# Down matmuls and small transforms as crossed pairs of 64-row halves

## The chip, the cores and the metric

The kernel runs on one core of a Trainium2 chip, in one launch. The metric is the device time of that launch in microseconds, as the median of several runs; before the change it is 916.47 us (three runs, 916.1 to 916.57). All matmul operands are bf16, all sums are kept in float32 in PSUM. The engines are called as the profile calls them: PE (TensorE), PEld (its weight loads), DVE (VectorE), ACT (ScalarE), POOL (GpSimd), SP (which issues DMAs).

## What is computed

A sequence of 2048 tokens with 576 channels passes through two layers, each of which is a long-convolution block A and then a gated feed-forward block B, both with a residual:

```python
def _A_ref(q, k, v, shift_k, ssm_k, ssm_D):
    k_shift = ...            # causal 4-tap filter of k, by channel
    kv = k_shift * v
    y = ...                  # causal convolution of kv with ssm_k over 2048 steps (by FFT)
    y = y + kv * ssm_D[None, None, :]
    return q * y

def _B_ref(x, w_gate, w_up, w_down):
    return (_gelu(x @ w_gate) * (x @ w_up)) @ w_down

x = A_q
x = x + _A_ref(_layernorm(x, axis=-1), A_k, A_v, A_shift_k, A_ssm_k, A_ssm_D)
x = x + _B_ref(_layernorm(x, axis=-1), B_w_gate, B_w_up, B_w_down)
x = x + _A_ref(_layernorm(x, axis=-1), A_k, A_v, A_shift_k, A_ssm_k, A_ssm_D)
x = x + _B_ref(_layernorm(x, axis=-1), B_w_gate, B_w_up, B_w_down)
```

The gate and up matrices are 576 x 4608, the down matrix 4608 x 576. The convolution's result does not depend on the layer's input, so it is computed once and used in both layers.

## The kernel before

**Units, passes and visits.** The tokens are cut into four chunks of 512 (four rows of 128). A unit is one layer on one chunk; there are eight, in five passes (`passes = [[0], [1, 2], [3, 4], [5, 6], [7]]`, L750). The 4608 hidden columns are cut into three phases of 12 tiles of 128. A visit is one phase of one unit, 24 visits in all (loop from L1569). In each visit PE first runs gate/up and then down.

**Gate/up** (`gu`, L1038): the contraction over 576 channels is cut into nine blocks of 64. Gate's block lies on partitions 0 to 63 and up's on 64 to 127, so a gate matmul of 64 rows and an up matmul of 64 rows run side by side in the two halves of the array, each 512 columns long and into its own PSUM bank. For each of the 12 tiles `fi` this is nine pairs. ACT then applies gelu, DVE multiplies and writes `hT` (L1619 to L1629).

**Down** (loop from L1643): for each of the four rows `j` and each tile `fi`, two matmuls of the full 128 rows and 288 columns (the two halves `h` of the 576 outputs, `down`, L1650) accumulate in a tile of two PSUM banks. A row is finished before the next is begun. Its result is added to the residual by DVE, in `plus` (queued in `late`, L1698) or directly for the second layer's last phase.

**PSUM.** There are four tiles of two banks (L760). Three are handed out in turn by `pr` (L784), which notes in `bank_at` when each will be free; the fourth belongs to the convolution's transforms, which may also borrow one of the three (`other`, `conv.alt`).

**Transforms.** While the units run, the convolution of chunks 1 to 3 is worked off beside them: the Fourier transforms are small matmuls on PE, `quarter` (L307) and `fwd_eo` (L295) forward and `inverse` (L347) back, each with 128 rows and 288 columns. ACT or DVE evicts them (the forward ones into `eo`, of which there are few), DVE combines them (`cross`, L318). They stand in the queue `Pq` and are issued by `run_p` (L709) within `fill` (L1099).

**The order of work** is written by the program itself: it keeps a clock for PE, DVE and ACT (`Pace`), with a fixed cost for every kind of operation (constants at L32 to L43), and issues each piece of other work into the engines' queues when the clocks say that it fits. `fill` is called after every gate/up tile and after every down tile; it issues loads, evictions, gate and norm steps on DVE (`run_vq`, L1007) and ACT (`run_aq`, L894), convolution work on DVE and transforms on PE. Between gate/up tiles a transform is issued only if two can go together or it has been skipped twice (`pair_ready`, L699), and then `C_TURN = 0.2` us is added to PE's clock (L1641). `pressing` (L1093) says that the next unit's input is due soon. Each engine runs its instructions in the order in which they were issued; waits between engines are semaphores that the framework derives from the tiles read and written.

The normalised rows of a unit are transposed either by a DMA on SP's queue (`spread`) or on PE (`turn_row`, L1049).

Of the kernel before, what the change touches and what calls it, by code (L numbers as in the profile page):

```python
# [17 lines left out]
P = 128  # L18
# [3 lines left out]
RT = BS // P  # L22
HW = 288
# [3 lines left out]
NEVER = 1e9  # L27
# [6 lines left out]
C_P0, C_P1, C_AC = 1.28, 1.35, 0.7  # L34
C_TT, C_ST, C_BN, C_NORM, C_HT, C_GELU, C_EVA, C_EVD, C_YH = 0.69, 0.75, 0.47, 0.62, 0.615, 0.51, 0.56, 0.69, 0.7
C_HB = 0.345
C_FOLD = 0.38
C_TURN = 0.2
LAG = 0.25
AHEAD = 2.0  # L40
SLOW, PRESS = 6.0, 22.0
NAT = 22.0
HOLD, SOON, QUIET, LEAD, FAR = 18.0, 30.0, 10.0, 1.8, 3.6  # L43
# [91 lines left out]
class Conv:  # L135
# [9 lines left out]
    def __init__(self, tc, ctx, pace, gwork, xtp, A_k, A_v, A_shift_k, A_ssm_k, A_ssm_D, ident, cps, ypool):  # L145
# [40 lines left out]
        self.left = 0  # L186
        self.spills = deque()

# [106 lines left out]
    def fwd_eo(self, src, kt, s, h, ring, scale=1.0):  # L295

        nc = self.nc
        ps = self.ps()
        for e in range(2):
            for i in (e, e + 2):  # L300
                nc.tensor.matmul(ps[:, e, 0:HW], lhsT=self.fw(kt, s, i),  # L301
                                 rhs=src(i)[:, h * HW:(h + 1) * HW], start=(i == e), stop=(i == e + 2))
        eo = self.eo_tile(ring)
        nc.scalar.activation(out=eo[:], in_=ps[:, :, 0:HW], func=ACT.Copy, scale=scale)
        return eo

    def quarter(self, src, e, s, h, ring, scale=1.0):  # L307

        nc = self.nc
        ps = self.ps()  # L310
        for n, i in enumerate((e, e + 2)):
            nc.tensor.matmul(ps[:, n, 0:HW], lhsT=self.fw(0, s, i), rhs=src(i)[:, h * HW:(h + 1) * HW], start=True, stop=True)  # L312
        eo = self.eo_tile(ring)
        nc.scalar.activation(out=eo[:], in_=ps[:, :, 0:HW], func=ACT.Copy, scale=scale)  # L314
        return eo
# [31 lines left out]
    def inverse(self, m, mt, terms):  # L347
        nc = self.nc
        if m not in self.y:
            self.y[m] = self.ypool.tile([P, RT, self.D], BF16, tag="y", name="y")  # L350
        ps = self.ps()
        for n, (lhs, z) in enumerate(terms):
            for h in range(2):
                nc.tensor.matmul(ps[:, h, 0:HW], lhsT=lhs, rhs=z[:, h * HW:(h + 1) * HW],  # L354
                                 start=(n == 0), stop=(n == len(terms) - 1))
        return self.halves(self.y[m][:, mt, :]), ps[:, :, 0:HW]
# [19 lines left out]
    def step(self, m, kv=None, loaded=False):  # L376
# [74 lines left out]
        def fwd(kt, s, h):  # L451
            def run():
                if s == 0 and h == 0:
                    for k in (kt, kt + 2):
                        kc[k] = self.kcp.tile([P, 2, D], BF16, tag="kc", name="kc")
                free, ring = self.eo_free(True)
                eo = self.fwd_eo(lambda i: self.vt_[m][:, i, :], kt, s, h, ring)
                done = t.on_act(C_EVA, max(t.pe + 0.49 + LAG, self.eo_at[ring].popleft()))
                self.ps_free[self.cur] = done
                if (kt, s, h) == (1, 1, 1):  # L460
                    self.fwd_at[m] = t.pe + 0.49
# [109 lines left out]
        def fwd4(filt, e, s, h):  # L571
# [3 lines left out]
            def run():  # L575
                free, ring = self.eo_free(m == 1)
                eo = self.quarter(src, e, s, h, ring, scale)
                done = t.on_act(C_EVA, max(t.pe + 0.25 + LAG, self.eo_at[ring].popleft()))
                self.ps_free[self.cur] = done
                if last:  # L580
                    (self.hf_at if filt else self.fwd_at)[m] = t.pe + 0.25
                    if filt and loaded:
                        self.hr_free[0] = self.hr_free[1] = self.hf_at[m]
# [63 lines left out]
        def inv(mt):  # L647
            def run():
                self.yb = nyb
                cost = 0.49  # L650
                out, in_ = self.inverse(m, mt, [(self.V_[:, s, mt, :], w[mt, s]) for s in range(2)])
# [6 lines left out]
                self.ps_free[self.cur] = done + LAG  # L658
                self.y_at[(m, mt)] = done + LAG
            return run  # L660
# [48 lines left out]
    def run_p(self):  # L709
# [10 lines left out]
        self.Pq.popleft()  # L720
        run()
        t.pe += cost
        if self.cur:
            self.borrowed(self.ps_free[1])
        return True

@with_exitstack
def ssm_geglu_kernel(ctx, tc, A_q, A_k, A_v, A_shift_k, A_ssm_k, A_ssm_D, B_x, B_w_gate, B_w_up,
# [165 lines left out]
    def run_aq(limit):  # L894
        only = coming[0] if pressing() else None
        found = [(prio, n) for n, (prio, ready, cost, run, ui) in enumerate(aq) if (only is None or ui == only) and ready() <= t.pe]
        if not found:
            return False
        n = min(found)[1]
        cost, run = aq[n][2:4]  # L900
        if max(t.act, t.pe - 1.0) + cost > limit:
            return False
        del aq[n]
        run()
        return True
# [101 lines left out]
    def run_vq(limit):  # L1007
# [7 lines left out]
        else:  # L1015
            r = NEVER if len(xn_made) >= 3 or not xn_open() else need[1].get("rstd_at", NEVER)
        if r > t.pe + 0.2 or max(t.dve, t.pe - 1.0) + cost > limit:
            return False
# [50 lines left out]

    conv.borrowed = lambda when: bank_at.__setitem__(taken[0] % 3, when)  # L1070
    conv.alt_at = lambda: bank_at[(taken[0] + 1) % 3]
# [26 lines left out]

    def fill(limit, tensor, conv_first, between=None):  # L1099
        weights()  # L1100
        conv.run_loads()
        spreads(tensor=tensor)
        while True:
            if run_late(limit):
# [31 lines left out]
    with tc.manual_schedule():  # L1136
# [432 lines left out]
        for at, (wb, ph, ui, first, final) in enumerate(visits):  # L1569
            coming[0], due_at[0] = ui, t.pe  # L1570
            layer, c = units[ui]
            while xn_done.get(ui, 0) < RT:
                if xn_made and xn_made[0][3] - 0.3 <= t.pe:
                    turn_row(*xn_made.popleft())
# [67 lines left out]
            ahead[:] = [t.pe + RT * FP * C_DN, visits[at + 1][2] if at + 1 < len(visits) else None]  # L1642
            for j in range(RT):  # L1643
                acc = pr("dn")
                mine = taken[0]
                conv.alt = other
                xa = x_c[c][:, j, :]
                xh = xa.rearrange("p (h d) -> p h d", h=2)

                def down(fi, h, acc=acc):  # L1650
                    nc.tensor.matmul(acc[:, h, 0:HW], lhsT=hT[:, fi, j * P:(j + 1) * P],  # L1651
                                     rhs=wd[2 * wb + fi // WT][:, fi % WT, h * HW:(h + 1) * HW],
                                     start=(fi == 0), stop=(fi == FP - 1))
                if wb == NWB - 1 and j == RT - 1:
                    dst = out2[c * CH:(c + 1) * CH, :].rearrange("(p j) d -> p j d", j=RT)[:, j, :]
                    for h in range(2):
# [7 lines left out]
                        nc.sync.dma_start(out=dst[:, h * HW:(h + 1) * HW], in_=ob[:, 0:HW])  # L1664
                    break
                for fi in range(FP):
                    for h in range(2):
                        down(fi, h)
                    t.pe += C_DN
                    if fi < FP - 1:  # L1670
                        fill(t.pe + 1.5, True, conv.left > 0)
                if layer == 1 and end:
                    ob, entry = out_tile()
# [9 lines left out]
                else:  # L1683
                    def plus(c=c, j=j, layer=layer, ph=ph, end=end, acc=acc, xa=xa, xh=xh):
# [11 lines left out]
                        if layer == 0 and end:  # L1696
                            vq.extend(prep(units.index((1, c)), j))
                    late.append((t.pe + 0.2, mine, plus))  # L1698
        conv.flush(NEVER)

# [49 lines left out]
```

## Time and profile before

| | |
|---|---|
| median of three runs | 916.47 us |
| profiled execution | 916.83 us |
| its span, first to last instruction | 915.1 us |
| granted TensorE clock in the profiled execution | 1.0 |
| instructions in the span | 19163 |
| PE matmuls | 8051 |
| bytes moved by DMA | 128.81 MB, mean 141 GB/s |

The profile is of one execution. A row of its groups gives the line and engine, the output and inputs by the program's names, the shape and count, then the busy time in us, the mean duration of one in ns, and the idle time before them with what ended it. Matmuls overlap in the pipeline: one of 288 columns lasts 286 ns from start to end, and the next begins long before that, so the pitch from one to the next has to be taken from a stretch of many. In shapes, `64*128 64x512` is a matmul that uses 64 rows and 128 columns of the array and streams 512 columns. The chain is the sequence of work that ended last, followed back from the end; its pieces are given with start, length and count.

### The profile page before, as it was taken

The page shows a single profiled execution, that of the slowest core. Times are in us where ns is not written, and L with a number is a line of the kernel's source. Part 1 is how long each engine was busy: PE and PEld are TensorE (multiplying, and loading weights), DVE is VectorE, ACT ScalarE, POOL GpSimd, SP SyncE. Part 2 cuts the span into 40 slices and gives each one's busy share as a digit, 9 for nine tenths or more (in the row PEclk, how much of TensorE's full clock was granted, in tenths as well). Part 3 has the DMA queues.
Part 4 walks back from the last instruction along what each step waited for, and adds up shares of the span by engine and source line. Part 5 has one row for each costly group of instructions (what it writes and reads, how often), then busy time and mean ns, then how long its engine had stood idle before and what let it go on. Part 6 is the DMA issues. An engine that isn't in the chain of part 4 may idle for free.

```text
span 915.1 us, 19163 instructions
## 1 busy us (share of the span) xinstructions
PE 907.8 (99%) x8051; PEld 522.5 (57%) x8051; DVE 565.0 (62%) x1131; ACT 364.7 (40%) x679; POOL 148.4 (16%) x311
## 2 busy tenths in 40 slices
PE   9999999999999999999999999999999999999998
PEld 7746556465565564655655655646646546556555
DVE  8888987774889886578887833543333334433332
ACT  7774446535435366254244233441121224321211
POOL 5443003320113012231023001210000002100000
PEclk9999999999999999999999999999999999999999
DMA  9999967449619606986944700882720820877630
GB/s 245 307 250 271 247 157 127 128 135 230 200 53 231 140 1 98 253 131 161 240 143 92 167 16 27 145 154 57 139 78 1 155 79 14 150 164 179 134 101 27
DMA packets 125819, 128.81 MB, mean 141 GB/s; under 512 B 40866, under 2 KB 118051, under 8 KB 125732
## 3 DMA queue, kind: packets, MB, share of 16 engines
q1 hardware_dynamic: 116706, 92.63, 47.8%
q0 software_dynamic: 8880, 34.36, 11.9%
q8 instruction: 63, 1.03, 0.5%
q10 hardware_dynamic: 146, 0.59, 0.2%
q14 instruction: 24, 0.20, 0.1%
HBM read 106.91 MB, written 11.80 MB: 130 GB/s over the span
## 4 chain that ended last, share of the span: by engine, by line
PE 93%; DVE 4%; ACT 1%; issue 1%; POOL 1%; DMA 0%; ACTq 0%; DVEq 0%; SPq 0%
PE gu L1041 57%; PE dn L1651 30%; PE ps L284 1%; PE cps L312 1%; DVE kvt L255 1%; PE cps L354 1%; DVE kvt L261 1%; PE ps L1273 0%; PE cps L301 0%; DVE x_c L925 0%; DVE hT L1629 0%; PE ps L1408 0%; DVE hT L1621 0%; PE ps L1041 0%; DVE hh L610 0%
## 5 line engine op out<-in xcount | busy, mean ns | idle before, releaser
L1041 PE MATMUL gu<-xnT,wgu 64*128 64x512 bf16 x5148 | 560.6, 376 | 0.9 <-DVE hT L1629 0.6
L1041 PEld LDWEIGHTS <-wgu 64*128 64x128 bf16 x5220 | 252.4, 94 | 306.1 <-issue 7.0
L1651 PE MATMUL dn<-wd,hT 128*128 128x288 bf16 x2304 | 293.9, 286 | 0.0
L1651 PEld LDWEIGHTS <-hT 128*128 128x128 bf16 x2304 | 223.4, 98 | 65.8 <-issue 8.1
L1629 DVE TENSOR_TENSOR hT<-ga,gu 128x512 bf16<-128x512 f32 x169 | 115.7, 686 | 175.6 <-ACT ga L1628 175.5
L1628 ACT ACTIVATE ga<-gu 128x512 f32<-128x512 f32 x169 | 100.5, 595 | 309.4 <-PE gu L1041 305.6
L1619 ACT ACTIVATE ga<-gu 128x512 bf16<-128x512 f32 x117 | 69.8, 597 | 156.4 <-PE gu L1041 143.0
L1621 DVE TENSOR_TENSOR hT<-ga 128x512 bf16<-128x512 bf16 x118 | 49.3, 420 | 57.4 <-ACT ga L1620 57.3
L1620 ACT CAST ga<-gu 128x512 bf16<-128x512 f32 x117 | 67.9, 580 | 0.0
L873 POOL TENSOR_SCALAR means<-s 128x1 f32<-128x1 f32 x28 | 16.0, 573 | 238.1 <-DVE x_c L1687 211.1
L1695 DVE TENSOR_TENSOR x_c<-x_c,dn 128x576 f32<-128x576 f32 x32 | 24.0, 751 | 26.3 <-PE dn L1651 26.1
L1693 DVE SCALAR_TENSOR_TENSOR x_c<-dn,means,x_c 128x576 f32<-128x576 f32 x28 | 22.8, 814 | 26.2 <-PE dn L1651 26.2
L314 ACT ACTIVATE eo<-cps 128x576 f32<-128x576 f32 x40 | 25.3, 657 | 25.1 <-DVE ab L319 9.2
L889 POOL TENSOR_TENSOR rstd<-ve,neghalf_t 128x1 f32<-128x1 f32 x56 | 33.6, 600 | 4.7
L331 DVE TENSOR_TENSOR prod<-prod 128x576 bf16<-128x576 bf16 x64 | 29.3, 458 | 2.2
L1674 DVE TENSOR_TENSOR xn<-x_c,dn 128x576 bf16<-128x576 f32 x15 | 11.3, 753 | 28.0 <-PE dn L1651 28.0
L915 ACT ACTIVATE yh<-y,rstd 128x576 f32<-128x576 bf16 x28 | 21.3, 771 | 10.4 <-DVE x_c L925 8.1
L610 DVE TENSOR_TENSOR kc<-ab,cd 128x288 bf16<-128x288 f32 x64 | 25.2, 449 | 0.0
L873 POOL TENSOR_SCALAR nm<-s 128x1 f32<-128x1 f32 x28 | 9.9, 353 | 94.1 <-DVE x_c L925 94.0
L425 POOL DMA_DIRECT2D kr<-Kd x20 | 11.0, 551 | 83.8 <-DVE prod L330 83.8
L881 ACT ACTIVATE junk<-x_c,nm 128x576 bf16<-128x576 f32 x28 | 21.5, 767 | 4.0 <-POOL nm L873 2.8
L888 POOL TENSOR_SCALAR ve<-ss 128x1 f32<-128x1 f32 x56 | 15.2, 272 | 41.8 <-ACT junk L881 41.6
(177 smaller groups left out, 609.3 us busy)
## 6 DMA issues: line engine op xcount, KB each, us to landing
wgu<-in_B_w_gate_dram SPq DMA_DIRECT2D x45, 576.0 KB, 5.6
wd<-in_B_w_down_dram SPq DMA_DIRECT2D x30, 864.0 KB, 6.7
wgu<-in_B_w_up_dram SPq DMA_DIRECT2D x45, 512.0 KB, 8.3
hr<-Hd POOLq DMA_DIRECT2D x32, 288.0 KB, 5.4
kr<-Kd POOLq DMA_DIRECT2D x24, 288.0 KB, 4.3
Kd<-kc POOLq DMA_DIRECT2D x12, 288.0 KB, 5.9
k<-in_A_k_dram POOLq DMA_DIRECT2D x3, 1008.0 KB, 11.0
wgu<-in_B_w_up_dram SPq DMA_DIRECT2D x45, 64.0 KB, 7.6
```

The lines of the kernel that those rows point to most:

```text
L314: nc.scalar.activation(out=eo[:], in_=ps[:, :, 0:HW], func=ACT.Copy, scale=scale)
L331: nc.vector.tensor_tensor(out=dst[:, cols], in0=pr[:, 0, cols], in1=pr[:, 1, cols], op=ALU.subtract if part == 0 else ALU.add)
L610: nc.vector.tensor_tensor(out=into[k][:, plane, cols], in0=a, in1=b, op=op)
L873: nc.gpsimd.tensor_scalar(out=v["nm"][:], in0=v["s"][:], scalar1=-1.0 / D, scalar2=None, op0=ALU.mult)
L889: nc.gpsimd.tensor_tensor(out=v["rstd"][:], in0=ve[:], in1=neghalf_t[:, 0:1], op=ALU.pow)
L1041: nc.tensor.matmul(cols(pair[:, s, :]), lhsT=w[r0:r0 + HK, k, gi * P:(gi + 1) * P], rhs=cols(xnT[r0:r0 + HK, blk_of[k], :]), start=(k == 0 ...
L1619: nc.scalar.activation(out=ga[:, 0, :], in_=pair[:, 0, :], func=ACT.Gelu_apprx_tanh)
L1620: nc.scalar.copy(out=ga[:, 1, :], in_=pair[:, 1, :])
L1621: nc.vector.tensor_tensor(out=hT[:, fi, :], in0=ga[:, 0, :], in1=ga[:, 1, :], op=ALU.mult)
L1628: nc.scalar.activation(out=ga[:], in_=pair[:, 0, :], func=ACT.Gelu_apprx_tanh)
L1629: nc.vector.tensor_tensor(out=hT[:, fi, :], in0=ga[:], in1=pair[:, 1, :], op=ALU.mult)
L1651: nc.tensor.matmul(acc[:, h, 0:HW], lhsT=hT[:, fi, j * P:(j + 1) * P], rhs=wd[2 * wb + fi // WT][:, fi % WT, h * HW:(h + 1) * HW], start=( ...
```

## The change

Matmuls with 128 contraction rows are split into two of 64 rows each, as gate/up has them. A tile has two output halves in two banks. In step 0 the upper 64 rows go to the first output and the lower 64 to the second, side by side; in step 1 crossed, the lower rows to the first output and the upper to the second. Between the steps a wait is placed: an empty instruction on ACT's sequencer that reads the PSUM tile (`conv.hold`), so that step 1 begins on PE only when step 0 has been written.

```diff
+    def half_rows(self, outs, terms, step):
+        for n, (lhs, rhs) in enumerate(terms):
+            for k in range(2):
+                r = slice((step ^ k) * (P // 2), (step ^ k) * (P // 2) + P // 2)
+                self.nc.tensor.matmul(outs[k], lhsT=lhs[k][r], rhs=rhs[k][r], start=step == 0 and n == 0,
+                                      stop=step == 1 and n == len(terms) - 1)
+
+    def both_steps(self, outs, terms):
+        ps = self.ps()
+        self.half_rows(outs(ps), terms, 0)
+        self.hold(ps)
+        yield
+        self.half_rows(outs(ps), terms, 1)
+        return ps
...
+    conv.hold = lambda ps: nc.scalar.keepalive_nop([nc.scalar.lower_ap(ps[:, :, 0:HW])])
```

`fwd_eo` and `quarter` use it, `inverse` too for chunks 2 and 3 (`m > 1`); for chunk 1 it stays as it was. `run_p` issues step 0 and puts the rest into a list `open`; `run_open`, called at the start of `fill`, issues step 1 when PE's clock is `DRAIN = 0.35` us further. Other matmuls stand between the two.

The down rows go two by two; the last two rows of the last visit stay whole and one by one:

```diff
+            def two_rows(j):
+                order = ([(0, 0, fi) for fi in range(FP - 2)] + [(1, 0, fi) for fi in range(FP - 3)] +
+                         [(0, 0, fi) for fi in range(FP - 2, FP)] + [(1, 0, fi) for fi in range(FP - 3, FP)] +
+                         [(n, 1, fi) for n in range(2) for fi in range(FP)])
+                for k, (n, step, fi) in enumerate(order):
+                    acc, mine = opened(j + n)
...
+                    for g in range(2):
+                        r = slice((step ^ g) * HK, (step ^ g) * HK + HK)
+                        nc.tensor.matmul(acc[:, g, 0:HW], lhsT=lhs[r], rhs=wn[r, g * HW:(g + 1) * HW],
+                                         start=step == 0 and fi == 0, stop=step == 1 and fi == FP - 1)
+                    if step == 0 and fi == FP - 1:
+                        conv.hold(acc)
+                    t.pe += C_DN / 2
+                    if step == 1 and fi == FP - 1:
+                        evict(j + n)
+                    elif k % 2:
+                        conv.alt = other
+                        fill(t.pe + 1.5, True, conv.left > 0)
...
+            two_rows(0)
+            if wb == NWB - 1:
+                conv.alt = None
+                row(2)
+                row(3)
+            else:
+                two_rows(2)
```

So of two rows, the first one's step 0 runs for ten tiles, the second one's for nine, then the first one's last two and the second one's last three, and then step 1 of the first row and of the second.

The planner's numbers and rules change with it: `C_TT` 0.69 to 0.74, `C_ST` 0.75 to 0.80, `C_EVD` 0.69 to 0.72, `C_TURN` 0.2 to 0.0, `SLOW` 6.0 to 5.0, a transform's matmuls count half for each step; between gate/up tiles `pair_ready` is no longer asked; while the next unit is `pressing`, steps of it may be issued up to `NEAR = 2.2` us before they are ready, and `run_aq` is called before DVE's work then and otherwise once instead of repeatedly:

```diff
-        while run_aq(min(limit, t.pe + 2.3)):
-            pass
+        run_aq(min(limit, t.pe + 2.3))
         conv.between = between is not None
-        if tensor and between is not None and not ((1 in conv.z_at or conv.dry(between)) and conv.pair_ready()):
+        if tensor and between is not None and not (1 in conv.z_at or conv.dry(between)):
             return
```

More of the change, by code (lines that the diff above doesn't have):

```diff
@@ L649, in run @@
                 self.yb = nyb
-                cost = 0.49
-                out, in_ = self.inverse(m, mt, [(self.V_[:, s, mt, :], w[mt, s]) for s in range(2)])
+                cost, cur = 0.25 if m > 1 else 0.49, self.cur
+                out, in_ = yield from self.inverse(m, mt, [(self.V_[:, s, mt, :], w[mt, s]) for s in range(2)])
                 if max(t.dve, t.pe + cost) < max(t.act, t.pe + cost):
@@ L720, in run_p, with run_open @@
         self.Pq.popleft()
[L721 to L724, printed above, removed]
-        return True
+        run = run()
+        if next(run, "whole") == "whole":
+            t.pe += cost
+            if self.cur:
+                self.borrowed(self.slot(), self.ps_free[1])
+            return True
+        self.ps_free[self.cur] = NEVER
+        t.pe += cost / 2
+        self.open.append((t.pe + DRAIN, cost / 2, run, self.cur, self.slot()))
+        return True
+    def run_open(self, now):
+        while self.open and self.open[0][0] <= now:
+            _, cost, run, cur, place = self.open.popleft()
+            for _ in run:
+                pass
+            self.t.pe += cost
+            if cur:
+                self.borrowed(place, self.ps_free[1])
 @with_exitstack
@@ L895, in run_aq @@
         only = coming[0] if pressing() else None
[L896 removed]
+        found = [(prio, n) for n, (prio, ready, cost, run, ui) in enumerate(aq) if (only is None or ui == only) and ready() <= t.pe + (0.0 if only is None else NEAR)]
         if not found:
@@ L1642, in ssm_geglu_kernel, with opened, row, down @@
             ahead[:] = [t.pe + RT * FP * C_DN, visits[at + 1][2] if at + 1 < len(visits) else None]
[L1643 to L1650, printed above, removed]
+            accs = {}
+            def opened(j):
+                if j not in accs:
+                    accs[j] = pr("dn"), taken[0]
+                return accs[j]
+            def row(j):
+                acc, mine = opened(j)
+                xh = x_c[c][:, j, :].rearrange("p (h d) -> p h d", h=2)
+                def down(fi, h, acc):
                     nc.tensor.matmul(acc[:, h, 0:HW], lhsT=hT[:, fi, j * P:(j + 1) * P],
```

87 lines of the change are left out of this document (54 added, 33 removed).

## The prediction

> **What bounds the kernel now.** I read the page's busy shares, its chain and its groups first, then the list of PE's waits, then the chain in order of time, and last the timeline of PE inside one visit.
>
> ```profile
> span 915.1 us, 19163 instructions
> PE 907.8 (99%) x8051; PEld 522.5 (57%) x8051; DVE 565.0 (62%) x1131; ACT 364.7 (40%) x679; POOL 148.4 (16%) x311
> PE 93%; DVE 4%; ACT 1%; issue 1%; POOL 1%; DMA 0%; ACTq 0%; DVEq 0%; SPq 0%
> L1041 PE MATMUL gu<-xnT,wgu 64*128 64x512 bf16 x5148 | 560.6, 376 | 0.9 <-DVE hT L1629 0.6
> L1041 PEld LDWEIGHTS <-wgu 64*128 64x128 bf16 x5220 | 252.4, 94 | 306.1 <-issue 7.0
> L1651 PE MATMUL dn<-wd,hT 128*128 128x288 bf16 x2304 | 293.9, 286 | 0.0
> L1651 PEld LDWEIGHTS <-hT 128*128 128x128 bf16 x2304 | 223.4, 98 | 65.8 <-issue 8.1
> ```
>
> TensorE sets the time: it is busy for 99% of the span and makes 93% of the chain, and two groups, gate/up (gu) and down (dn), are 854.5 of its 907.8 us. Its waits are few:
>
> ```profile
> PE ps L1186 <- DVE ones L1158: 1.1, 1, 1.1
> PE cps L312 <- ACT eo L314: 0.7, 1, 0.7
> PE cps L312 <- ACT ga L1620: 0.6, 1, 0.6
> PE gu L1041 <- DVE hT L1629: 0.6, 1, 0.6
> PE ps L1514 <- DVE xn L1500: 0.5, 2, 0.3
> PE gu L1041 <- DMA xnT<-xn: 0.3, 1, 0.3
> ```
>
> That is 3.8 us in all. So nothing but PE's own stream can give much, and the streaming itself stays: a dn row of 12 tiles is 24 matmuls of 288 columns now, and 24 pair-steps of 288 columns afterwards. What is left is the seam between the two kinds of matmul. It shows when a steady stretch is held against a whole one:
>
> ```profile
> 138.51 1.09 PE cps L354 x8
> 139.60 2.05 PE gu L1041 x18
> ...
> 268.79 23.42 PE gu L1041 x216
> 292.21 11.87 PE dn L1651 x96
> ...
> 545.42 0.98 PE cps L354 x8
> ```
>
> ```profile
> 269.81 20.45 PE L1041 MATMUL gu<-xnT,wgu 64*128 64x512 bf16 x188
> 292.76 10.45 PE L1651 MATMUL dn<-wd,hT 128*128 128x288 bf16 x84
> ```
>
> Inside gu, 94 pairs take 20.45 less the last one's 0.38, over 93 steps: 0.2158 us a pair, so 108 pairs are 23.31; the chain has 23.42. Inside dn, (10.45 - 0.286) / 83 = 0.1225, so 96 are 11.76; the chain has 11.87. Each run pays 0.11 us once, where PE passes from 64-row to 128-row matmuls or back. The inverse transform says the same: its 8 matmuls take 1.09 between gu runs, 0.98 between dn runs.
>
> **What the change removes.** In PE's order of instructions, from the first gate/up on, the matmuls change between 64 and 128 rows 55 times before and 9 times after (the two double inverses of block 1 inside gu, two transposed rows inside dn, and one at the whole rows of the last visit). 46 x 0.11 = 5.1 us less. The startup, before the first gate/up, is unchanged.
>
> **What the pairs cost.** 64-row pairs of 288 columns are not in the trace, but longer and shorter ones are. The pitch could be bound by issue or by weight loads, four instructions per pair-step instead of two:
>
> ```profile
> L1041 PE MATMUL ps<-xnT,wgu x72: 269/269/279, 40.3 to 44.1; 64*128 64x256 bf16 x72
> ...
> 40.83 2.35 PE L1041 MATMUL ps<-xnT,wgu 64*128 64x256 bf16 x40
> ```
>
> 20 pairs of 256 columns: (2.35 - 0.27) / 19 = 0.1093 us a pair. Issue and loads thus manage at least one pair in 0.109, below the 0.1225 that 288 columns stream. The loads agree: 252.4 us for 2610 pairs is 0.097 a pair, since the two halves load side by side. I take no extra pitch. Each nanosecond of it on some 2,400 pair-steps would cost 2.4 us.
>
> **Crossings.** Where a step changes, the half that came second in one pair comes first in the next, so the same 64 rows are used twice running. After the startup that happens 208 times.
>
> ```profile
> 269.81 0.38 PE L1041 MATMUL gu<-xnT,wgu 64*128 64x512 bf16 x2
> ```
>
> A pair of 0.376 us matmuls takes 0.38, so the second starts about 0.004 behind. A crossing should lose just this offset: 208 x 0.0035 = 0.7 us. Lower bound 0 (all dn rows now reuse the same rows back to back at 0.1225); upper bound the price of a seam, 0.11, that is 23 us. I take the small one because the dn row is the nearest. The Trainium skill, page "TensorE: Matmul & The Clock Gate", Part 3, "The mechanism", speaks against this: a weight load overlaps a running matmul only when the row group differs, and by that rule every crossing would expose a load, 208 x 0.094 = 19.6 us. The dn group disagrees, with 0.098 us loads on the same rows hidden in a pitch of 0.1225; no run here shows it for halves that swap.
>
> **The holds.** Between step 0 and step 1 of a tile stands a wait: ScalarE's sequencer waits for the last matmul of step 0 and then releases PE. There are 94 in dn and 56 in small transforms; PE waits on 143 of them. What the wait must cover: the matmul's own 0.286, then PE to ScalarE, the event itself, and ScalarE to PE.
>
> ```profile
> 290.75 1.46 PE L1041 MATMUL gu<-xnT,wgu 64*128 64x512 bf16 x12
> 292.25 0.60 ACT L1619 ACTIVATE ga<-gu 128x512 bf16<-128x512 f32 x1 [0.87 <-PE gu L1041]
> ```
>
> ```profile
> L1619 ACTq EVENT_SEMAPHORE  x110: 17/17/17, 44.4 to 511.2; - x110
> ...
> 174.25 0.69 DVE hT L1629
> 174.94 0.04 issue
> 174.98 1.02 PE gu L1041 x7
> ```
>
> 0.04 (292.21 to 292.25), 0.02 and 0.04 (here from VectorE to PE) make about 0.39 us. In dn the tight hold, that of the first row of two, has three pair-steps of the other row between: step 1 is due 4 x 0.1225 = 0.49 after the last matmul of step 0 began. The second row's is due after 1.6 us. So both are hidden while ScalarE's sequencer is free, with 0.10 to spare on the tight one. PE's instructions behind the wait, weight loads among them, then arrive late: I allow 0.01 for each of some 47 tight holds, 0.5 us (bounds: 0, and 47 x 0.11 = 5.2 if each restart costs what a seam does).
>
> ScalarE is not always free. A hold stands behind earlier evictions of transforms (eo), and those wait for VectorE to free their buffer:
>
> ```profile
>   DVE ab L319: 9.2, 6
>   DVE cd L319: 6.0, 5
> ...
>   DVE kc L319: 1.7, 1
> ```
>
> These are the waits ended by VectorE, 16.9 us in 12, up to 3 us each; today PE stands behind such an eviction once (0.7 us, above). A hold counts only if it stands right behind such an eviction and step 1 falls due before it ends. In the first transform stretch after the hand-over the evictions ran so:
>
> ```profile
> 186.78 0.65 ACT L314 ACTIVATE eo<-cps 128x576 f32<-128x576 f32 x1 [1.58 <-PE dn L1651]
> 189.91 0.65 ACT L314 ACTIVATE eo<-cps 128x576 f32<-128x576 f32 x1 [2.48 <-PE dn L1651]
> 193.51 1.39 ACT L314 ACTIVATE eo<-cps 128x576 f32<-128x576 f32 x2 [2.95 <-DVE ab L319]
> ```
>
> They are 3 us apart while a hold has its answer within about 0.6 of its step 0, and PE's own wait lets VectorE catch up. I take 0.5 us for all of them (bounds 0 and 16.9).
>
> **Hand-over.** After the second double inverse PE meets the wait for transposed rows of the next unit (0.3 above) whatever it saves in front of it: the two seams of that stretch, 0.2 us, turn into waiting. The two waits on ScalarE near the start, 0.6 and 0.7, stay: the same gelu copies and evictions end them, and a hold's delay is taken out of the next wait. DMA order moves little (a pair of transposed rows and one down-weight load change places on SP's queue), and both down rows of a pair have a bank free before they open. The planner's retuned costs shift some VectorE and ScalarE instructions by a few places; PE's stream covers that, since these engines are busy for 62% and 40%, and where the cover is thin, early, the second rival prices it. I take 0 for these.
>
> **Sum.** -5.1 + 0.7 + 0.5 + 0.5 + 0.2 = -3.2 us. The profiled execution took 916.83 (span 915.1 and 1.7 around it), so 913.6; it lay 0.36 above the median of 916.47, so **913.3** as a median.
>
> **Rivals.**
> A hold is where this goes wrong on the other side (slower). If half of the 16.9 us of eviction waits come to stand before PE, less 0.1 of cover in each of 6, that is 7.8 instead of 0.5: -3.2 + 7.3 = +4.1, **920.6**. It decides, against the forecast's 3.2 us, from 3.7 us on. For it: ScalarE's sequencer takes its instructions in order, and the waits are long. Against it: few fall due close together, and ScalarE is busy for only 40% of the span.
>
> The gain of the early part is absorbed. Between 44 and 235 us VectorE is nearly as loaded as PE:
>
> ```profile
> 44.00:235.00 191.00, 188.83 (x1662) 108.08 (x1658) 151.89 (x332) 99.43 (x191) 43.02 (x77) 1.00 0.81 190
> ```
>
> Of the 46 seams 10 lie there, net: PE arrives 1.1 us sooner and waits for what VectorE has not finished. With 1.5 us of waits in place of the 0.5 and the 0.2, the other 36 x 0.11 = 4.0 stand against 0.7 + 0.5 + 1.5: -1.3, **915.2**.
>
> Crossings cost a weight load: -3.2 - 0.7 + 0.094 x 208 = +15.7, **932.2**. For it only that swapped halves appear nowhere in the trace.
>
> The change doesn't do what it says, because the 0.11 belongs to starting another kind of run and not to the number of rows: then no 5.1, and +1.7 from the new terms, **918.2**.
>
> **How the numbers follow.** Forecast 0.55, absorbed 0.18, holds 0.15, no seam saved 0.06, crossings 0.06. The measurement tells 0.2%, 1.8 us, from no change: faster means below 914.6, slower above 918.3. The forecast's own range is 911.4 to 915.0 (extra cover for holds, or restarts at double my price). Faster: nearly all of the forecast and a little of the absorbed case, 0.57. Same: most of the absorbed case and half of the no-seam one, 0.21. Slower: holds, crossings and the rest, 0.22. The range for 8 in 10 is 911.0 to 920.0; crossings and the worst of the holds lie outside.
>
> **What would show it.** Right: in the chain gu pieces of 23.3 us and dn pieces of 11.8 with 192 matmuls; the dn group at 64 rows with twice the count and a pitch of 0.1225 a pair; PE's list of waits without a line for ScalarE's sequencer above 1 us. Holds exposed: lines of dn or cps waiting for the ACT queue, and short dn pieces in the chain between 65 and 420 us. Crossings: a dn piece of 12.1 us or more (4 x 0.094 more) in a visit without transforms. A pitch above 0.1225 inside one step would make the prediction wrong at its root.

## The result, and the profile after

| | before | after |
|---|---|---|
| median of seven runs each | 916.52 us | 913.47 us |
| span of the profiled execution | 915.1 us | 911.5 us |
| PE matmuls | 8051 | 10451 |

The ratio of after to before is 0.9967, with a 95% interval of 0.9957 to 0.9977. The change makes the kernel 3.05 us faster. The forecast was 913.3.

The page of the profile after, its first lines, the chain's shares and the gate/up and down groups (columns as before):

```profile
span 911.5 us, 24246 instructions
PE 904.0 (99%) x10451; PEld 600.2 (66%) x10451; DVE 565.1 (62%) x1129; ACT 363.2 (40%) x675; POOL 146.8 (16%) x311
...
PE 94%; DVE 4%; ACT 1%; issue 1%; POOL 0%; ACTq 0%
...
L1081 PE MATMUL gu<-xnT,wgu 64*128 64x512 bf16 x5148 | 561.0, 376 | 1.1 <-DVE hT L1674 0.9
L1735 PE MATMUL dn<-wd,hT 64*128 64x288 bf16 x4512 | 294.6, 283 | 0.8 <-ACTq L1110 0.4
L1735 PEld LDWEIGHTS <-hT 64*128 64x128 bf16 x4512 | 253.3, 94 | 28.7 <-issue 1.6
```

PE still sets the time, busy for 99% of the span as before. The down group has twice the matmuls, less the two rows that stay whole, and the same streaming: 4512 of 64 rows and 48 of 128 in place of 2304. Its weight loads are twice as many and are busy for 253.3 us instead of 223.4, not for twice as long: 4512 loads of 0.094 would be 424 us one after the other, so the two halves load side by side for a good part. The groups cannot show where 3 us went; the chain can. First the chain of before in order of time (start, length, piece), then that of after:

```profile
196.26 23.42 PE gu L1041 x216
...
415.80 23.42 PE gu L1041 x216
...
558.90 23.42 PE gu L1041 x216
...
876.45 23.42 PE gu L1041 x216
```

```profile
138.44 2.05 PE gu L1081 x18
...
194.44 23.31 PE gu L1081 x216
...
266.89 23.31 PE gu L1081 x216
290.20 11.76 PE dn L1735 x192
...
413.95 23.31 PE gu L1081 x216
...
557.31 23.31 PE gu L1081 x216
...
872.94 23.31 PE gu L1081 x216
```

Every visit in which only gu and dn run is some 0.21 us shorter: gu 23.31 instead of 23.42, dn 11.76 instead of 11.87. Those are the two figures that the prediction had worked out from pitch times count, with no seam left in them. Setting the same gu pieces of the two chains against each other gives the gain as it builds up: 1.16 us at the second piece of 18 (139.60 to 138.44), 1.82 at 196, 1.90 at 269, 1.85 at 416, only 1.59 at 559, and from there 0.21 a visit (nine visits) to 3.51 at 876. So the gain grows evenly where nothing but gu and dn runs, does not grow between 196 and 416 although seams are saved there too, and is thrown back between 416 and 559. PE's waits after tell part of it (what was waited for: us in total, times, longest):

```profile
PE ps L1230 <- DVE ones L1202: 1.1, 1, 1.1
PE gu L1081 <- DVE hT L1674: 0.9, 1, 0.9
PE ps L1558 <- DVE xn L1544: 0.5, 2, 0.3
PE dn L1735 <- ACTq L1110: 0.4, 1, 0.4
PE cps L310 <- ACTq L1110: 0.4, 1, 0.4
PE dn L1735 <- DVE x_c L1771: 0.3, 2, 0.2
```

The first and third lie in the startup and stood there before. Before, the others were 0.7 and 0.6 on ScalarE, 0.6 on hT and 0.3 on the transposed rows; after, they are 0.9 on hT, twice 0.4 on a hold (ACTq L1110) and 0.3 on x_c: 2.2 before and 2.0 after.

This list undercounts. It takes the idle time from the end of the last matmul to the start of the next, but a dn matmul lasts 0.283 us and the next pair is due 0.1225 after its start (0.376 and 0.2158 in gu). So each wait costs PE 0.16 us more than is listed, and a start that is less than that late isn't in the list at all. Read from the starts of single matmuls against these pitches, the late starts that are not seams, from the first gate/up tile on, make 3.05 us before and 4.4 after: 1.3 us more waiting, at other places.

The 0.9, by the starts 1.12, is the step back at 527 us. The timeline of after there (start, length, engine and line, operation; idle time before it in brackets):

```profile
523.32 0.45 DVE L559 TENSOR_TENSOR w<-yb 128x576 bf16<-128x576 bf16 x1
...
526.76 0.46 DVE L560 TENSOR_TENSOR yb<-yb 128x576 bf16<-128x576 bf16 x1
527.14 2.09 DVE L1674 TENSOR_TENSOR hT<-ga,gu 128x512 bf16<-128x512 f32 x3
527.87 1.47 PE L1081 MATMUL gu<-xnT,wgu 64*128 64x512 bf16 x12 [0.94 <-DVE hT L1674]
```

Eight fold steps of the convolution (L559 and L560 by turns, from the first row to the second), each 0.49 us after the last, stand ahead of the multiply that frees gate/up's banks. The planner counts 0.38 for one (`C_FOLD`, L37), so after eight it believes VectorE about 0.9 us further on than it is, which is near what PE then waits.

One of the two holds in the list shows the mechanism that the prediction priced as its slower rival. The chain of after between 183 and 186 us:

```profile
183.71 0.75 DVE cd L334 x2
...
184.48 0.02 ACTq L329
...
184.62 0.05 ACT eo L329
...
184.71 1.40 PE dn L1735 x20
```

A down row's step 1 waits for its hold; the hold stands on ScalarE's sequencer behind an eviction into eo (L329), and that eviction waits for VectorE's combining step (cd, L334), which frees the eo buffer. By the starts it costs 0.58 us, and it happens once. The other hold of the list, at 66 us, makes 0.55; in the chain it stands on ScalarE behind a sum for the normalisation (L919) and a gelu (L1664), so behind other work than was priced. A third start behind a hold, at 335 us, is 0.10 late.

### The profile page after: what moved, and what is told of

Same layout as the page of the kernel before. It is cut to its first block, busy times and chain, and to the rows that moved or that the text cites. A ratio compares the mean times of both kernels' runs of the same rounds, so it can differ in the third digit from the quotient of the medians.

```text
span 911.5 us, 24246 instructions
## 1 busy us (share of the span) xinstructions
PE 904.0 (99%) x10451; PEld 600.2 (66%) x10451; DVE 565.1 (62%) x1129; ACT 363.2 (40%) x675; POOL 146.8 (16%) x311
## 4 chain that ended last, share of the span: by engine, by line
PE 94%; DVE 4%; ACT 1%; issue 1%; POOL 0%; ACTq 0%
PE gu L1081 58%; PE dn L1735 29%; PE cps L310 2%; PE ps L284 2%; DVE kvt L255 1%; PE dn L1701 1%; DVE kvt L261 1%; DVE kc L633 0%; PE ps L1317 0%; DVE hT L1666 0%; DVE cd L334 0%; PE ps L1452 0%; PE ps L1081 0%; DVE hh L633 0%; POOL rstd L1537 0%
## 5 line engine op out<-in xcount | busy, mean ns | idle before, releaser
L1081 PEld LDWEIGHTS <-wgu 64*128 64x128 bf16 x5220 | 293.5, 94 | 262.3 <-issue 2.3
L1735 PE MATMUL dn<-wd,hT 64*128 64x288 bf16 x4512 | 294.6, 283 | 0.8 <-ACTq L1110 0.4
L1735 PEld LDWEIGHTS <-hT 64*128 64x128 bf16 x4512 | 253.3, 94 | 28.7 <-issue 1.6
L1673 ACT ACTIVATE ga<-gu 128x512 f32<-128x512 f32 x175 | 104.4, 597 | 318.9 <-PE gu L1081 312.7
L1674 DVE TENSOR_TENSOR hT<-ga,gu 128x512 bf16<-128x512 f32 x175 | 120.0, 686 | 172.5 <-ACT ga L1673 172.0
L1664 ACT ACTIVATE ga<-gu 128x512 bf16<-128x512 f32 x111 | 66.2, 597 | 148.4 <-PE gu L1081 140.6
L1666 DVE TENSOR_TENSOR hT<-ga 128x512 bf16<-128x512 bf16 x112 | 46.9, 421 | 54.7 <-ACT ga L1665 54.7
L1665 ACT CAST ga<-gu 128x512 bf16<-128x512 f32 x111 | 64.4, 580 | 0.0
L911 POOL TENSOR_SCALAR means<-s 128x1 f32<-128x1 f32 x28 | 16.9, 606 | 245.1 <-DVE x_c L1765 216.8
L1771 DVE SCALAR_TENSOR_TENSOR x_c<-dn,means,x_c 128x576 f32<-128x576 f32 x28 | 22.8, 815 | 24.5 <-PE dn L1735 24.4
L329 ACT ACTIVATE eo<-cps 128x576 f32<-128x576 f32 x40 | 25.6, 657 | 21.3 <-PE cps L310 16.7
L911 POOL TENSOR_SCALAR nm<-s 128x1 f32<-128x1 f32 x28 | 7.9, 281 | 94.8 <-DVE x_c L965 94.7
L919 ACT ACTIVATE junk<-x_c,nm 128x576 bf16<-128x576 f32 x28 | 21.5, 767 | 4.0 <-POOL nm L911 3.5
L955 ACT ACTIVATE yh<-y,rstd 128x576 f32<-128x576 bf16 x28 | 21.2, 768 | 2.3 <-PE dn L1735 1.4
L449 POOL DMA_DIRECT2D hr<-Hd x32 | 17.6, 551 | 21.4 <-DVE prod L345 19.9
```

Of the source, the lines that this page charges most:

```text
L911: nc.gpsimd.tensor_scalar(out=v["nm"][:], in0=v["s"][:], scalar1=-1.0 / D, scalar2=None, op0=ALU.mult)
L1081: nc.tensor.matmul(cols(pair[:, s, :]), lhsT=w[r0:r0 + HK, k, gi * P:(gi + 1) * P], rhs=cols(xnT[r0:r0 + HK, blk_of[k], :]), start=(k == 0 ...
L1664: nc.scalar.activation(out=ga[:, 0, :], in_=pair[:, 0, :], func=ACT.Gelu_apprx_tanh)
L1665: nc.scalar.copy(out=ga[:, 1, :], in_=pair[:, 1, :])
L1666: nc.vector.tensor_tensor(out=hT[:, fi, :], in0=ga[:, 0, :], in1=ga[:, 1, :], op=ALU.mult)
L1673: nc.scalar.activation(out=ga[:], in_=pair[:, 0, :], func=ACT.Gelu_apprx_tanh)
```

## The experiments

**The changed kernel again, without crossings, with crossings everywhere, and with more seams.** These four ran on one chip against the same runs of the kernel before (916.67 us). The first is the changed kernel as it is, for a base.

> The changed kernel once more, as the yardstick of the three beside it. Expected as in the result: some 3.0 us below the kernel before, 913 to 914 us.

Measured: 913.29 us, ratio 0.9968 [0.9955, 0.998].

In the second, step 1 issues its two halves in the other order, so that no half of the array is used twice running:

```diff
-            for k in range(2):
+            for k in (step, 1 - step):
...
-                    for g in range(2):
+                    for g in (step, 1 - step):
```

> In step 1 the matmul of the upper 64 rows is issued first, so that the halves alternate everywhere: 208 crossings become none; seams (9) and holds (150) stay. Offset theory (a crossing loses the 0.0035 us by which the second half starts late): 0.7 us less than the changed kernel. If a crossing costs nothing: the same time within 0.2 us. If a crossing exposed a weight load (0.094 us): 19.6 us less, which the steady dn pieces of 11.76 us already speak against.

Measured: 913.21 us, ratio 0.9965 [0.9951, 0.9979]. The third goes to the other end: the order of halves is turned over at every pair-step, so that 2209 pairs begin with the half that the pair before ended with, instead of 208:

```diff
-            for k in range(2):
+            for k in ((n + step) % 2, (n + step + 1) % 2):
...
-                    for g in range(2):
+                    for g in (k % 2, 1 - k % 2):
```

> The half that is issued first changes at every pair-step of the split matmuls: 2209 crossings in place of 208, all else equal. Offset theory: 2001 x 0.0035 = 7 us more than the changed kernel and a dn pitch of 0.126 us a pair. If a crossing costs nothing: the same time and a pitch of 0.1225. If it exposes a load: some 190 us more.

Measured: 913.43 us, ratio 0.9966 [0.9954, 0.9979], and a dn piece in its chain as long as in the changed kernel:

```profile
255.05 11.76 PE dn L1735 x192
```

Two thousand more crossings cost 0.14 us, which is within the scatter of the runs. A crossing is free: neither the offset of 0.0035 us (7 us for 2001 more) nor an exposed weight load of 0.094 us (188 us) is there. The rule of the Trainium skill, page "TensorE: Matmul & The Clock Gate", Part 3, "The mechanism", that a load overlaps a running matmul only on another row group, is not borne out for halves that swap either.

In the fourth, rows 2 and 3 of every visit run whole, one by one, as before:

```diff
-                if j == RT - 1:
+                if wb == NWB - 1 and j == RT - 1:
...
-                two_rows(2)
+            conv.alt = None if wb == NWB - 1 else other
+            row(2)
+            if wb < NWB - 1:
+                conv.alt = other
+            row(3)
```

> The third and fourth down row of every visit run whole, with 128 rows, one by one, as before the change; the first two rows and the transforms stay in halves. 115 changes between 64 and 128 rows in place of 9, 104 holds in place of 150. Seam theory (a change of rows costs 0.11 us wherever it stands): 106 x 0.11 = 11.7 us more than the changed kernel, so some 8 us above the kernel before. Rival (the 0.11 belongs to passing from gate/up to down, of which there are as many as before the change): 46 such passages at most, 5 us more or less.

Measured: 922.18 us, ratio 1.0061 [1.0049, 1.0074], 8.9 us more than the base. The chain has the seams at their places:

```profile
265.47 5.99 PE dn L1701 x48
271.46 23.42 PE gu L1081 x216
294.87 5.88 PE dn L1735 x96
300.75 5.99 PE dn L1701 x48
```

48 whole matmuls are 48 x 0.1225 = 5.88 and take 5.99; gu is back at 23.42; the halved rows keep 5.88. The 106 more seams at 0.106 us, the excess of these pieces when it is read from the starts of single matmuls, make 11.2 us. The 2.3 us between are waits that this kernel doesn't have: the late starts of the changed kernel at 226, 335 to 340, 370, 408 and 527 us, 2.4 us in all, are on time here.

**Nearer and further holds, the old planner, and the fold's cost.** These four ran on one chip too (before: 916.59 us). A tight hold has three pair-steps of the other row behind it. Here it has one:

```diff
-                order = ([(0, 0, fi) for fi in range(FP - 2)] + [(1, 0, fi) for fi in range(FP - 3)] +
-                         [(0, 0, fi) for fi in range(FP - 2, FP)] + [(1, 0, fi) for fi in range(FP - 3, FP)] +
+                order = ([(0, 0, fi) for fi in range(FP - 2)] + [(1, 0, fi) for fi in range(FP - 1)] +
+                         [(0, 0, fi) for fi in range(FP - 2, FP)] + [(1, 0, fi) for fi in range(FP - 1, FP)] +
```

> In a pair of down rows the second row runs eleven tiles of step 0 before the first row's last two, so that one pair-step instead of three stands between the first row's last step 0 and its step 1, which is then due after 2 x 0.1225 = 0.245 us instead of 0.49. Hold theory (a hold takes 0.39 us from the start of the awaited matmul to the release of PE): 0.145 us exposed in each of 47 tight holds, 6.8 us more than the changed kernel, some 920 us. If a hold takes less than 0.245 us: the same time. If each exposed wait also costs a restart of 0.1 us: 11.5 us more.

Measured: 919.97 us, ratio 1.0037 [1.0025, 1.005]: slower than before. A visit's dn piece in its chain:

```profile
291.45 12.09 PE dn L1735 x192
```

Two holds in a visit make 12.09 - 11.76 = 0.33, so 0.165 each. Step 1 was due 2 x 0.1225 = 0.245 after the last matmul of step 0 began, so the whole way from that matmul through ScalarE's sequencer and back takes 0.41 us. The prediction had put it together from rows of before to 0.39. The pair that has waited is followed by the next one 0.121 us later, which is the usual pitch, so there is no cost of a restart on top. By the starts 43 of the 47 tight holds are exposed, 7.1 us in all; the kernel is 6.7 above the changed one, since some small waits of that one are shorter here. Now with six pair-steps behind the hold instead of three (FP - 6 for FP - 3 in both places):

> The second row runs six tiles of step 0 before the first row's last two, so that six pair-steps stand between in place of three: step 1 is due after 0.86 us. Hold theory with the 0.49 us already covering (down pieces of 11.76 us are as long as their pitch alone): the same time within 0.3 us. If the tight holds still cost 0.01 us each: 0.5 us less. Rival: the first row's last two tiles, now 0.37 us earlier, wait for the gelu of the last gate/up tiles, some 0.1 us or more in each of 23 visits: 2 us or more above the changed kernel.

Measured: 913.2 us, ratio 0.9965 [0.9951, 0.9978], with dn pieces of 11.76 as before it. More cover gives nothing that can be told (0.1 us), so with 0.49 us of cover for 0.41 the tight holds already cost nothing.

The change also retunes the planner. Undone alone, with the halves kept:

```diff
-C_TT, C_ST, C_BN, C_NORM, C_HT, C_GELU, C_EVA, C_EVD, C_YH = 0.74, 0.80, 0.47, 0.62, 0.615, 0.51, 0.56, 0.72, 0.7
+C_TT, C_ST, C_BN, C_NORM, C_HT, C_GELU, C_EVA, C_EVD, C_YH = 0.69, 0.75, 0.47, 0.62, 0.615, 0.51, 0.56, 0.69, 0.7
...
-SLOW, PRESS = 5.0, 22.0
-NAT, NEAR = 22.0, 2.2
+SLOW, PRESS = 6.0, 22.0
+NAT, NEAR = 22.0, 0.0
...
-        if r > t.pe + (NEAR if pressing() else 0.2) or max(t.dve, t.pe - 1.0, r) + cost > limit:
+        if r > t.pe + 0.2 or max(t.dve, t.pe - 1.0, r) + cost > limit:
...
-        while pressing() and run_aq(min(limit, t.pe + 2.3)):
-            pass
...
-        run_aq(min(limit, t.pe + 2.3))
+        while run_aq(min(limit, t.pe + 2.3)):
+            pass
```

> The halves and holds as in the changed kernel, but the planner's costs C_TT, C_ST, C_EVD and SLOW, the calls of run_aq and the readiness of run_vq as before the change; C_TURN stays 0 and pair_ready stays out. 11 seams in place of 9. Seam theory: within 1 us of the changed kernel. Rival (the retuned planner carries the gain, by keeping holds and evictions out of PE's way): 2 us or more above it.

Measured: 915.54 us, ratio 0.9989 [0.998, 0.9997], some 2.2 us over the changed kernel: a miss, since less than 1 us was expected, and the rival's "2 us or more" is the number that came. The halves with the old planner are only 1.05 us faster than the kernel before. PE's list of waits shows one cause, a wait on ScalarE, which its timeline puts near 65 us; by the starts it is 1.13 there, against 0.33 in the changed kernel:

```profile
PE cps L310 <- ACT ga L1664: 0.9, 1, 0.9
```

The wait on hT at 527 us is in its list as well (0.9), so the retuning did not bring that one.

Last of the four, the fold's cost at what the trace shows:

```diff
-C_FOLD = 0.38
+C_FOLD = 0.49
```

> The planner's cost of one fold step, C_FOLD, from 0.38 to the 0.49 us from one to the next in the trace (524.30 to 524.79). If the one long wait of the changed kernel (PE on VectorE's hT, 0.9 us at 527, where eight fold steps stand before hT) comes from this: 1.1 us less than the changed kernel, 912.3 us. If it comes from another cost: the same time, with the wait in the same place.

Measured: 912.23 us, ratio 0.9954 [0.9941, 0.9966], about 1 us faster than the changed kernel, each held against the kernel before on its own chip; the wait at 527 us is worth 1.12 by the starts. The line for hT is gone from PE's waits, and in the timeline a multiply for hT now stands after the fourth fold step.

**Whole transforms, halved inverses, and the old rules alone.** These three ran together (before: 916.75 us). First the down rows in halves, but the transforms of the running convolutions whole, at the place of their step 1:

```diff
-        self.half_rows(outs(ps), terms, 0)
-        self.hold(ps)
         yield
-        self.half_rows(outs(ps), terms, 1)
+        for n, (lhs, rhs) in enumerate(terms):
+            for k in range(2):
+                self.nc.tensor.matmul(outs(ps)[k], lhsT=lhs[k], rhs=rhs[k], start=n == 0, stop=n == len(terms) - 1)
```

> The changed kernel, but the transforms of the running convolutions use all 128 rows again, at the place in PE's order where step 1 stood; only the down rows stay in halves. The matmuls then change between 64 and 128 rows 121 times instead of 9, most of them inside down rows. Theory (a change of rows costs 0.106 us wherever it lies, and halving only the down rows would be worse than not halving at all): 112 x 0.106 = 11.9 us more than the changed kernel, about 925, less some 2 us if PE's few stalls disappear in the added time; the chain shows transform pieces of 0.98 + 0.11 for 8 matmuls. Rival (the gain comes from the down rows being in halves and taken two by two, the transforms don't matter): 913 to 914.

Measured: 922.64 us, ratio 1.0064 [1.0049, 1.008], some 9.3 us over the changed kernel. Its chain, and that of the changed kernel in the same stretch, show why:

```profile
187.08 0.35 PE cps L319 x2
187.43 2.31 PE dn L1735 x36
```

```profile
189.54 0.12 PE cps L310 x2
189.66 0.49 PE dn L1735 x8
```

A transform of two matmuls takes 2 x 0.12 = 0.24 us as two pair-steps among dn in halves, and 0.35 whole: one seam more. The other falls into the dn piece that follows, 2.31 us for 18 pairs that stream 18 x 0.1225 = 2.21. 112 x 0.106 is 11.9; the list of waits has lost both holds and x_c, and the starts at 340 and 370 us are on time, which takes back most of the difference. Halving the down rows alone makes the kernel 0.6% slower than before: the gain needs both.

Next the fold's cost together with the inverses of block 1 in halves (`m > 0` for `m > 1` in both places), so that 7 seams are left:

> The changed kernel with C_FOLD at 0.49 (912.2 alone) and also the inverses of block 1 in halves, so that 7 changes of rows are left instead of 9. Theory: 2 x 0.106 = 0.2 us less, plus or minus what the planner's new order does to PE's few stalls (0.5): 911.5 to 912.5, not to be told from the kernel with C_FOLD alone; the stall at 526 us stays away. Rival (the removal of the stall by C_FOLD was an accident of one order and any other edit brings such stalls back): 913 or more, with a stall on the hT multiply above 0.5 us.

Measured: 912.55 us, ratio 0.9954 [0.9941, 0.9966], not to be told from the fold's cost alone, and no wait on hT. It has one more row transposed on PE than the changed kernel. In the groups, first the changed kernel, then this one:

```profile
L1097 PE MATMUL cps<-ident,xn 128*128 128x128 bf16 x18 | 1.4, 220 | 0.0
```

```profile
L1097 PE MATMUL cps<-ident,xn 128*128 128x128 bf16 x27 | 2.0, 220 | 0.0
```

The planner's clocks have sent that row to PE instead of a DMA: 0.6 us of matmuls and two seams, 0.8 in all, against the 0.4 that the inverses' four seams gave. Last, the planner's rules of before with the retuned costs kept, to split the miss on the planner:

> The changed kernel with the planner's scheduling rules of before (NEAR 0, SLOW 6, ScalarE's jobs in a loop at the end of fill, none at its beginning) and the retuned costs (C_TT, C_ST, C_EVD) kept. With rules and costs of before it took 915.54, 2.2 us more than the changed kernel. Theory (the rules carry it: ScalarE's other work is put ahead of a gelu or an eviction and PE waits for it near 65 us): 915 to 916, with the wait of the transform's bank on ScalarE of about 0.9 us near 65. Rival (the three costs carry it): 913.0 to 913.9 and a wait near 65 us of 0.6 or less.

Measured: 914.76 us, ratio 0.9979 [0.997, 0.9988]. Both theories miss: the time lies between their ranges, 1.4 us above the changed kernel where the whole old planner is 2.2, and the place is wrong in the first. The wait on ScalarE near 65 us is short:

```profile
PE cps L310 <- ACT ga L1664: 0.2, 1, 0.2
```

That wait goes with the three costs (0.9 with the old ones). What the rules carry is in part the row: this kernel and the one with the whole old planner also have 27 transposing matmuls on L1097, 0.6 us, and two seams, 0.2. Both also have one more start behind a hold, 0.25 late near 147 us, where the hold stands on ScalarE behind a step (yh, L955) that waits for VectorE. That makes 1.05; the profiled span is 0.9 longer than the changed kernel's, the median 1.4.

## Why the prediction was right

The total was right within 0.2 us, and so was the mechanism that carries it: the seams. That the rest came out near the +1.9 forecast for it (+1.3 by PE's starts) is in part luck: of its terms several were mis-sized, and they offset each other. With the old planner, whose retuning was priced at nothing, the same halves gain 1.05 us instead of 3.05.

- **Seams, -5.1.** Right. Where a steady visit can be read, gu and dn are the 23.31 and 11.76 that were worked out; 106 and 112 seams put in again cost 8.9 and 9.3 us. At 0.106 instead of 0.11 the 46 are 4.9 us.
- **Pitch of 64-row pairs of 288 columns, no extra cost.** Right: 11.76 / 96 = 0.1225. The margin was smaller than worked out: 253.3 us of loads for 2256 pairs are 0.112 a pair, not the 0.097 read from gate/up before.
- **Crossings, +0.7.** The step that failed is "A crossing should lose just this offset". It loses nothing, not with 2209 of them. The lower bound, from the dn rows that reuse the same rows back to back, was the better row.
- **Tight holds, +0.5.** The latency was nearly right (0.41 measured, 0.39 worked out); the allowance of 0.01 each was not needed, as the kernel with more cover shows.
- **Holds behind busy evictions, +0.5.** Right in kind, but too small: the holds at 66, 184 and 335 us make 1.2 us by the starts (the first of them lies in the early stretch, which is the subject of a point below). Only that at 184 is the chain DVE cd, eo, hold, PE that was described. The rival built on it was far off, though: it would have needed 3.7 us before PE, and of the 16.9 us of eviction waits on VectorE, ScalarE's list after has 6.7 in 7, with this line as the longest:

```profile
ACT eo L329 <- DVE cd L334: 4.2, 3, 1.8
```

- **Hand-over, +0.2.** "PE meets the wait for transposed rows of the next unit (0.3 above) whatever it saves in front of it" failed. The wait for the transposed rows (0.3) and that on hT behind it (0.6) are gone, 0.48 and 0.72 by the starts, and the chain of after has a gu piece there without a break:

```profile
159.25 21.37 PE gu L1081 x198
```

In the traces the first normalised row is made at 148.83 instead of 150.43, 1.6 us earlier, while PE reaches the new unit 1.2 us earlier (157.03 instead of 158.23). The chain of before had it already:

```profile
142.73 2.07 PE gu L1041 x18
144.82 0.61 ACT ga L1628
...
150.43 0.59 DVE xn L954
...
156.32 2.56 DMA xnT<-xn
```

It runs from PE's own last gate/up of the visit in front through ScalarE and VectorE to the transposes, so the rows' date was not a fixed one and moves with PE. Why it moved by 0.4 more was not tried.
- **The two early waits on ScalarE, 0.6 and 0.7, "stay".** Nearly right. In the list only one hold of 0.4 is left of that stretch, but by the starts PE is late by 1.7 us there before and by 1.4 after, now in five pieces of 0.12 to 0.55, the hold's 0.55 among them.
- **The planner's retuned costs, 0.** The step that failed is "PE's stream covers that". Undoing them and the rules with them costs 2.2 us. And the shifted order puts eight fold steps ahead of a multiply at 527 us, where the prediction saw no thin cover because it looked for that early only: 0.9 in the list, about 1 by the kernel that repairs it. Since that wait is there with the old costs and rules too, it comes from the halves, or from the rules for transforms that changed with them; no run separates these.
- **"Both down rows of a pair have a bank free before they open", 0.** Not quite. At 226 us a row's first pair waits for the eviction of the tile (x_c, L1771), 0.17 in the list:

```profile
225.17 1.16 PE L1735 MATMUL dn<-wd,hT 64*128 64x288 bf16 x16
...
225.63 0.81 DVE L1771 SCALAR_TENSOR_TENSOR x_c<-dn,means,x_c 128x576 f32<-128x576 f32 x1
...
226.50 0.67 PE L1735 MATMUL dn<-wd,hT 64*128 64x288 bf16 x8 [0.17 <-DVE x_c L1771]
```

Eight pairs from 225.17 on have had their turn at 225.17 + 8 x 0.1225 = 226.15; the next begins at 226.50, 0.35 late. The wait occurs twice. At 340 and 370 us it is too short for the list: there a gate/up tile and a down row start 0.21 and 0.19 late, 0.05 after VectorE has ended the eviction of a down row, and PE waits there for the same VectorE semaphore as at 226:

```profile
369.71 0.75 DVE L1752 TENSOR_TENSOR xn<-x_c,dn 128x576 bf16<-128x576 f32 x1
```

```profile
340.51 0.08 DVE L1765 DVE_READ_ACCUMULATOR x_c<-dn,x_c 128x1 f32 x1
```

Together the four make 1.1 us, where the prediction had none; before, no start after 175 us is late by more than 0.03 but for seams.

Of the rivals, no seam saved and crossings at a load's price are excluded by the runs. The early part was not absorbed in the way described, since the gain at 196 us is 1.8; but between 196 and 416 us, where six visits should give another 1.3 by the steady rate, it does not grow. That is the four bank waits, 1.1, and 0.15 at 335 to 338 us. The two short ones show in the chain as pieces longer than 23.31 and 5.88:

```profile
340.64 23.49 PE gu L1081 x216
...
370.51 6.06 PE dn L1735 x96
```

Summed by the starts: -4.9 for 46 seams, -1.2 at the hand-over, -0.25 for the early stretch and -0.15 for a start at 153 us that was late before; +0.6 for the hold at 184, +1.1 for bank waits, +0.15 at 335 to 338 and +1.1 at the fold. That is -3.55 against 3.6 less in the span, so nothing of size is left over. No run tried the early stretch or the hand-over by themselves.

## What to carry to other kernels

When a kernel's engine is 99% busy, hold a steady stretch against pitch times count: what is left over at each change of kind is a price that a count of changes turns into a forecast, and here it was right to 0.01 us for each piece. Bring all the work between two such changes into one form, or none: half of it in the new form (the down rows without the transforms) made the kernel 6 us slower than before instead of 3 faster. And where a planner with fixed costs orders the other engines, check its costs against the trace in the stretches where several of one kind go one after the other; one number set right gave 1 us more, a third of the whole change. Where matmuls overlap, read what a wait costs from the starts against the pitch, not from the list of idle times: here the list had less waiting after the change, and the starts 1.3 us more.

The best of the kernels run is the changed one with `C_FOLD` at 0.49: 912.23 us, 0.9954 of before. The halved inverses on top of it give nothing that can be told.

## What the runs showed of the hardware

- Passing between matmuls of 64 and of 128 rows costs PE 0.106 us each way, between gu and dn, inside a down row and around a transform alike.
- Two 64-row matmuls on the same half running, with swapped order, cost nothing: 2001 more of them changed the time by 0.14 us. The weight loads of 0.094 us stay hidden, at 0.112 us of loads in each pitch of 0.1225.
- The way from a matmul's start through an empty instruction on another engine's sequencer and back to PE is 0.41 us, of which the matmul's own is 0.28. The pair behind the wait is followed at the usual pitch. With 0.49 us of other work behind it, it is free; with 0.245, it costs 0.165.
